# Semaphore waits of VectorE's SBUF operations for GpSimd's

## Chip, core and metric

One core of a Trainium2 chip runs the whole program in one launch. The metric is the device time in microseconds; 947.63 us is the median of three runs of the kernel before.

## What is computed

Decay attention over 4 x 8 heads, 576 positions and head size 64, and behind it two MoE-like blocks of 2304 tokens (512 to 2048 to 512), all in float32:

```python
scores = scale * q @ k.T + cum[i] - cum[j]      # cum = cumsum(log(clip(f))), causal
attn = softmax(scores); x = (attn @ v).reshape(2304, 512)
h = x @ w_in;  g = where(h >= 1, h, where(h <= -1, 0, (h + 1) ** 2 / 4));  x = g @ w_out
h = x @ w_in2; P = a0 + a1 h + a2 h^2 + a3 h^3
Q = 1 + |b0| |h| + |b1| h^2;  out = (P / (Q + 1e-6)) @ w_out2
```

## The kernel before

Matrix products run in float32r as three passes over high and low parts: each float32 operand is copied (high part, ScalarE) and the rest is subtracted (low part, VectorE or GpSimd). The first part of the program, to about 216 us, works through 16 pairs of heads with nine blocks of rows each: TensorE writes scores to PSUM (S), GpSimd masks the decay tile (`cb`, `affine_select`), VectorE adds it and takes maxima (P, nm), ScalarE takes exponentials, TensorE transposes (T), VectorE or ScalarE copies to SBUF (PT), TensorE multiplies by v (O), and GpSimd scales the result (`xa`, by R, which comes by DMA). Beside that, weights are converted from float64 words (`raw` to `wd`: one step of ScalarE, four of VectorE on SBUF) and the first columns of MoE 1 are computed as filler. From 216 to about 540 us MoE 1 runs, then MoE 2, which takes seven products for eight and evaluates its rational function on ScalarE, VectorE and GpSimd.

The order of all this is not that of the loops. Each piece is given as a `task` (key, engine or several ways, duration, function, dependencies, buffers). `plan` (L325) lists the tasks greedily on a clock of its own, and `emit` (L1200) calls their functions in that order, so each engine's queue has the order of the list. A task on VectorE that works on SBUF alone has the way "dvp"; this and GpSimd's "pool" are `SHARED`, and the planner lets only one of them run at a time (`port`). When it lists a GpSimd task whose start is under `NEAR` = 1.0 behind the end of the last "dvp" task, it notes this task in `behind` (L371 to L376). `emit` then adds a dependence with a semaphore: the first GpSimd instruction of the task waits for the last VectorE instruction of the other (L1206, L1207). `Kept` records what each of the two engines is given. In the other direction the kernel before has no such wait: a "dvp" task listed behind a GpSimd task starts as soon as its own data are there. The plan is made twice, for attention with the filler and for the rest.

```python
                if eng == "pool" and lastv and at - lastv[1] < NEAR:
                    behind[n] = lastv[0]
                elif eng == "dvp":
                    lastv = n, at + dur
```

The tasks named in the steps below: `w_steps` (L102, conversion, `wd`), `split_x_lo` (`xl`), the low parts of q and k (`ql`, `kl`, `lo`) and the diagonal copies (`qdh`, `qdl`, `diag`), `mask_fn` (`cb`), `r6` (`xa`), `split_g_lo` (`gl`) and `q_add` (`h<-h,us`). All of VectorE's and GpSimd's instructions bear line L26, that of the recording helper, so the rows are told apart by tiles.

Of the kernel before, what the change touches and what calls it, by code (L numbers as in the profile page):

```python
# [32 lines left out]
def kernel(ctx, tc, qT, kT, v, f, w_in1, w_out1, w_in2, w_out2, a, b, out):  # L33
    nc = tc.nc
    PE, ACT, DVE, POOL, SP = nc.tensor, nc.scalar, Kept(nc.vector), Kept(nc.gpsimd), nc.sync
# [259 lines left out]
    port = [T0]  # L295
# [6 lines left out]
    NEAR = 1.0  # L302
    behind, given_to = {}, {}
    after_it = mybir.DependencyInfo(mybir.DependencyClass.Sync, mybir.DependencyReason.SCHED_ONLY)
# [20 lines left out]
    def plan(first, wk):  # L325
        left, users = {}, {}
        for n in range(first, len(tasks)):
            users.setdefault(n, [])
            left[n] = 0
            for d in tasks[n][2]:  # L330
                if d >= first:
                    users.setdefault(d, []).append(n)
                    left[n] += 1
        ready = {n for n, k in left.items() if k == 0}
        order = []
        lastv = None
        while ready:
            best = None
            for n in ready:
                key, ways, deps, take, _ = tasks[n]  # L340
                free_at = 0.0
                ok = True
                need = {}
                for tag in take:
                    k = need[tag] = need.get(tag, 0) + 1
                    if len(bufs[tag]) < k:
                        ok = False
                        break
                    free_at = max(free_at, sorted(bufs[tag])[k - 1])
                if not ok:  # L350
                    continue
                choice = None
                for w, (eng, dur, _) in enumerate(ways):
                    at = max(clock[OF.get(eng, eng)], free_at, port[0] if eng in SHARED else 0.0)
                    eng = OF.get(eng, eng)
                    for d in deps:
                        e2 = by[d]
                        at = max(at, done[d] + (0.13 if e2 == eng and eng != "pe" else 0.0 if e2 == eng else LAT[e2]))
                    end = at + dur if len(ways) > 1 else 0.0
                    if choice is None or end < choice[0]:  # L360
                        choice = (end, at, w)

                turn = SWC if ways[0][0] == "pe" and shape.get(n) != at_shape[0] else 0.0
                cand = (choice[1] + turn + wk * key, key, n, choice[1], choice[2])
                if best is None or cand < best:
                    best = cand
            assert best, [(tasks[n][0], tasks[n][3]) for n in ready]
            _, key, n, at, w = best
            _, ways, _, take, free = tasks[n]
            eng, dur, fn = ways[w]  # L370
            if eng in SHARED:  # L371
                port[0] = at + dur
                if eng == "pool" and lastv and at - lastv[1] < NEAR:
                    behind[n] = lastv[0]
                elif eng == "dvp":
                    lastv = n, at + dur  # L376
            eng = OF.get(eng, eng)
            ready.discard(n)
            by[n] = eng
            for tag in take:  # L380
                bufs[tag].remove(min(bufs[tag]))
            if eng == "sp":
                for issue, moved in dur:
                    dma[0] = max(dma[0], at) + issue
                    dma[1] = max(dma[1], dma[0] + 0.64) + MOVE * moved
                clock[eng] = dma[0]
                done[n] = dma[1] + LAND
            elif eng == "init":
                done[n] = dur
            else:  # L390
                if eng == "pe" and shape.get(n) != at_shape[0]:
                    at_shape[0] = shape.get(n)
                    dur += SWT
                clock[eng] = at + dur
                done[n] = at + dur
            for tag in free:
                bufs[tag].append(done[n] + LAT[eng])
            order.append((at, n, fn))
            for u in users[n]:
                left[u] -= 1  # L400
                if left[u] == 0:
                    ready.add(u)
        assert len(order) == len(left), (len(order), len(left))
        order.sort(key=lambda t: t[:2])
        return [t[1:] for t in order]
# [737 lines left out]
    for size, kind, x, k in pieces:  # L1143
        key = FS + (FE - FS) * sofar / whole
        sofar += size
        n = CH[x]
# [27 lines left out]
    for kk in range(KD):  # L1174
        n = CH[FILL]
# [23 lines left out]

    def emit(order):  # L1200

        for n, fn in order:
            DVE.given, POOL.given = [], []
            fn()
            given_to[n] = DVE.given
            if n in behind and POOL.given and given_to[behind[n]]:  # L1206
                tc.add_manual_dep(POOL.given[0].ins, given_to[behind[n]][-1].ins.name, after_it, reason="port")  # L1207

    bufs.update({tag: [T0] * n for tag, n in N_BUF.items()})
    nudge(0)  # L1210
    order_ = plan(0, WK)
    emit(order_)
    filling = False
    att.close()
# [88 lines left out]
    for p, (m, x, fs) in enumerate(passes):  # L1303
        n = CH[x % NCH]
# [71 lines left out]
    n = QN  # L1376
# [102 lines left out]
    for n, x in enumerate(2 * s + 1 - c for s in range(NSUP) for c in range(2)):  # L1479
        for g in range(NF):  # L1480
# [3 lines left out]
            for d in range(QN // P):  # L1484
# [4 lines left out]
                if g == NF - 1:  # L1489
                    eng = ("act", "dve")[d % 2]  # L1490
                    o = task(key, eng, cost(eng, DM, "ps"), lambda x=x, d=d, eng=eng: out_copy(x, d, eng), (tout,), (("d", "d", "t2")[d],), (f"a{d}",))
                    task(key, "sp", ld(DM), lambda x=x, d=d: out_store(x, d), (o,), (), (("d", "d", "t2")[d],))
    nudge(first)
    order_ = plan(first, WKB)
    emit(order_)
    man.close()

# [45 lines left out]
```

## Time and profile before

| | us |
|---|---|
| median of three runs | 947.63 (947.1 to 947.81) |
| the profiled execution | 947.7 |
| its span in the trace | 946.0 |
| TensorE busy | 933.5 |
| VectorE busy | 740.0 |
| ScalarE busy | 704.4 |
| GpSimd busy | 442.9 |

The profiled execution's own time is 1.7 us longer than its span, and lies among the three runs. Matmuls are pipelined, so a busy TensorE says that it is never without one, not that it is at its peak. A VectorE or GpSimd row has the start and the length of an instruction; time in which an instruction has started and can't go on counts as its length, not as idle time.

### The profile page before, as it was taken

What the parts mean: (1) busy time and instruction counts of PE and PEld (TensorE: products, weight loads), DVE (VectorE), ACT (ScalarE), POOL (GpSimd) and SP (SyncE); (2) the same over time, 40 slices, a digit from 0 to 9 for tenths busy, and PEclk for the clock granted to TensorE, in tenths of its full rate; (3) what the DMA queues carried; (4) which work ended last, traced back from release to release, by engine and by line L of the source; (5) the groups of instructions that cost most, each with busy time, mean ns of one, the idle gap of its engine ahead of it and who ended that gap; (6) DMA issues with size and microseconds to landing.
All of it is one profiled execution on the core that took longest, in us unless ns stands there. A gap on an engine that the chain in (4) does not pass through costs nothing.

```text
span 946.0 us, 16654 instructions
## 1 busy us (share of the span) xinstructions
PE 933.5 (99%) x5172; PEld 789.2 (83%) x5172; DVE 740.0 (78%) x1614; ACT 704.4 (74%) x1568; POOL 442.9 (47%) x542
## 2 busy tenths in 40 slices
PE   9899999999999999999999999999999999999998
PEld 5666877778888888888998888989898989998986
DVE  7989789873866987897558598899988888888840
ACT  7899888875765654655556599889988898878752
POOL 3655733635565222131322076666655556455553
PEclk9999999999999999999999999999999999999999
DMA  8789799846554477686948865867434363434100
GB/s 258 235 267 278 238 300 282 255 164 205 178 178 150 164 261 270 196 289 221 325 144 273 267 196 189 263 227 256 140 136 147 139 234 121 141 131 151 34 34 34
DMA packets 107345, 188.55 MB, mean 199 GB/s; under 512 B 13092, under 2 KB 43188, under 8 KB 107256
## 3 DMA queue, kind: packets, MB, share of 16 engines
q1 hardware_dynamic: 107256, 187.48, 59.9%
q8 instruction: 41, 0.67, 0.3%
q14 instruction: 48, 0.39, 0.1%
HBM read 142.72 MB, written 44.71 MB: 198 GB/s over the span
## 4 chain that ended last, share of the span: by engine, by line
PE 88%; DMA 4%; DVE 4%; ACT 1%; issue 1%; SPq 1%; POOL 0%; DVEq 0%; POOLq 0%
PE b L1077 21%; PE h L799 20%; PE h L1051 19%; PE a L901 19%; PE T L573 3%; PE O L610 3%; PE a L890 2%; PE S L507 2%; DVE P L26 1%; DMA cb<-cd 1%; DMA vt<-in_v_dram 1%; DMA raw<-in_moe_w_in_dram 1%; DVE wd L26 1%; PE S L498 1%; DVE PT L26 1%
## 5 line engine op out<-in xcount | busy, mean ns | idle before, releaser
L26 POOL TENSOR_TENSOR gl<-t,gh 128x512 fp32r<-128x512 f32 (+2 forms) x125 | 140.1, 1127 | 216.4 <-ACT gh L815 87.3
L1077 PE MATMUL b<-w,gh 128*128 128x512 f32 x576 | 179.1, 392 | 0.0
L901 PE MATMUL a<-gh,w 128*128 128x512 f32 (+1 forms) x576 | 161.7, 366 | 0.0
L26 POOL TENSOR_TENSOR t<-t,t 128x384 f32<-128x384 f32 x96 | 97.4, 1018 | 97.2 <-ACT t L847 77.4
L1077 PEld LDWEIGHTS b<-w,gh 128*128 128x128 f32 x576 | 108.0, 188 | 21.1
L26 DVE SCALAR_TENSOR_TENSOR t<-h,t 128x512 f32<-128x512 f32 (+2 forms) x125 | 73.6, 600 | 61.1 <-ACT t L831 60.5
L799 PE MATMUL h<-xh,arena 128*128 128x512 f32 (+1 forms) x400 | 119.7, 368 | 0.0
L901 PEld LDWEIGHTS a<-gh,w 128*128 128x128 f32 x576 | 104.0, 189 | 17.1
L1077 PE MATMUL b<-w,gl 128*128 128x512 f32 x288 | 112.0, 389 | 0.0
L815 ACT CAST gh<-t 128x512 fp32r<-128x512 f32 (+2 forms) x125 | 68.7, 553 | 49.5 <-PE a L901 25.4
L901 PE MATMUL a<-gl,w 128*128 128x512 f32 (+1 forms) x288 | 105.3, 366 | 0.0
L26 DVE SCALAR_TENSOR_TENSOR wd<-raw,wd 128x512 int32<-128x512 int32 x128 | 98.1, 767 | 2.6
L561 ACT ACTIVATE P<-P,nm 128x576 f32<-128x576 f32 (+2 forms) x144 | 83.6, 582 | 13.9 <-DVE nm L26 13.4
L1051 PE MATMUL h<-arena,q 128*128 128x384 f32 x459 | 93.3, 337 | 0.0
L826 ACT ACTIVATE t<-h 128x512 f32<-128x512 f32 (+1 forms) x77 | 42.5, 551 | 61.6 <-PE h L799 60.0
L1051 PEld LDWEIGHTS h<-arena,q 128*128 128x128 f32 x459 | 81.4, 188 | 4.5 <-DVE h L26 1.2
L26 DVE TENSOR_SCALAR wd<-wd 128x512 f32<-128x512 f32 (+1 forms) x128 | 66.9, 523 | 21.6 <-ACT wd L109 19.9
L799 PEld LDWEIGHTS h<-xh,arena 128*128 128x128 f32 x400 | 73.1, 189 | 12.4
L799 PE MATMUL h<-xl,arena 128*128 128x512 f32 (+1 forms) x200 | 73.6, 368 | 0.0
L26 DVE CUSTOM_DVE_ANT_0 P<-S,cb 128x256 f32<-128x256 f32 (+1 forms) x135 | 62.5, 477 | 11.4 <-POOL cb L26 4.9
L26 POOL TENSOR_SCALAR_AFFINE_SELECT cb<-cb 128x128 f32<-128x128 f32 (+1 forms) x150 | 43.4, 301 | 59.5 <-DVE wd L26 26.7
L573 PE MATMUL T<-ident,P 128*128 128x128 f32 x400 | 63.7, 281 | 6.6 <-DVE PT L26 4.0
(170 smaller groups left out, 2213.7 us busy)
## 6 DMA issues: line engine op xcount, KB each, us to landing
q<-wqd SPq DMA_DIRECT2D x46, 512.0 KB, 3.6
raw<-in_moe_w_in_dram SPq DMA_DIRECT2D x32, 512.0 KB, 5.0
raw<-in_moe_w_out_dram SPq DMA_DIRECT2D x32, 512.0 KB, 4.2
arena<-wqd SPq DMA_DIRECT2D x26, 512.0 KB, 3.5
cb<-cd SPq DMA_DIRECT2D x15, 576.0 KB
xr<-xd SPq DMA_DIRECT2D x32, 256.0 KB, 3.4
wqd<-t SPq DMA_DIRECT2D x32, 256.0 KB, 3.7
wfd<-wd SPq DMA_DIRECT2D x26, 256.0 KB
```

Source lines behind the costliest of these rows:

```text
L26: self.given.append(getattr(self.engine, name)(*args, **kwargs))
L507: PE.matmul(ts[jj][:, to], qq[pp, bb_ * P:(bb_ + 1) * P] if x < 3 else qq[pp, :], kk_[pp, 0:(bb_ + 1) * P], start=(x == 0 and bb_ == b), s ...
L561: ACT.activation(p, p, AF.Exp, scale=-1.0, bias=nm[pr][:, pos:pos + 1], accum_out=ls[pr][:, COL[pos]:COL[pos] + 1])
L573: PE.transpose(ps[:, (c - c0) * P:(c - c0 + 1) * P], p[:, k0:k0 + P], ident[:])
L610: PE.matmul(o[pp, c_q:n], nat[pr, 2][:, c, pp], pt[:, c, j, c_q:n], start=(c == 0), stop=(c == ncs - 1),)
L799: PE.matmul(hps[g], ww[:, kk * P:(kk + 1) * P], xx[kk], start=(kk == 0 and y == 0), stop=(kk == KD - 1 and y == 2))
L815: ACT.copy(gt[g][0], mid[g][0][:, 0:n])
L826: ACT.activation(s[:, 0:n], hps[g], AF.Relu, scale=0.5, bias=0.5)
L890: PE.matmul(acc[x, d], ww[:, dd], gg, start=(part == 0 and g == gs[0]), stop=(part == 2 and g == gs[-1]))
L901: PE.matmul(acc[x, d], ww[:, dd], gg, start=(first and y == 0), stop=(last and y == 2))
L1051: PE.matmul(o, ww, xx, start=(new and i == 0 and z == 0), stop=(i == HQ - 1 and z == 2), skip_group_check=True,)
L1077: PE.matmul(acc[x, d], gg[:, dd], ww, start=(g == 0 and y == 0), stop=(g == NF - 1 and y == 2))
```

## The change

The planner keeps the last listed task of both shared ways, and each new shared task that starts under `NEAR` behind the last one of the other engine is noted in `behind`. What was done for GpSimd's tasks is now done for "dvp" tasks too: their first VectorE instruction waits by a semaphore for the last GpSimd instruction of the task noted. The planner's choices don't depend on `behind`, so the list is the same.

```diff
-        lastv = None
+        last = {}
...
             if eng in SHARED:
                 port[0] = at + dur
-                if eng == "pool" and lastv and at - lastv[1] < NEAR:
-                    behind[n] = lastv[0]
-                elif eng == "dvp":
-                    lastv = n, at + dur
+                other = last.get("dvp" if eng == "pool" else "pool")
+                if other and at - other[1] < NEAR:
+                    behind[n] = other[0]
+                last[eng] = n, at + dur
...
         for n, fn in order:
             DVE.given, POOL.given = [], []
             fn()
-            given_to[n] = DVE.given
-            if n in behind and POOL.given and given_to[behind[n]]:
-                tc.add_manual_dep(POOL.given[0].ins, given_to[behind[n]][-1].ins.name, after_it, reason="port")
+            given_to[n] = DVE.given or POOL.given
+            if n in behind and given_to[n] and given_to[behind[n]]:
+                tc.add_manual_dep(given_to[n][0].ins, given_to[behind[n]][-1].ins.name, after_it, reason="port")
```

## Rows read from the trace of the kernel before

**Rows 1.** The page, busy us, share of the span, and instructions of each engine:
```profile
PE 933.5 (99%) x5172; PEld 789.2 (83%) x5172; DVE 740.0 (78%) x1614; ACT 704.4 (74%) x1568; POOL 442.9 (47%) x542
```
**Rows 2.** Busy time by stretch: length, each engine, granted clock, DMA share, GB/s:
```profile
24.00:57.00 33.00, 30.48 (x255) 21.39 (x255) 31.66 (x106) 29.50 (x90) 21.30 (x43) 1.00 0.74 239
57.00:92.00 35.00, 31.66 (x269) 22.63 (x266) 31.45 (x103) 33.69 (x101) 19.55 (x41) 1.00 0.89 275
92.00:140.00 48.00, 47.75 (x343) 38.17 (x341) 40.22 (x127) 42.34 (x116) 25.31 (x48) 1.00 0.86 272
140.00:216.00 76.00, 75.35 (x569) 57.24 (x567) 62.32 (x188) 61.65 (x177) 34.41 (x69) 1.00 0.72 229
216.00:540.00 324.00, 324.00 (x1611) 275.95 (x1610) 231.20 (x406) 190.77 (x354) 106.01 (x88) 1.00 0.66 223
540.00:900.00 360.00, 360.00 (x1806) 324.98 (x1805) 314.18 (x612) 312.64 (x662) 207.20 (x202) 1.00 0.50 168
```
**Rows 3.** Who waited for whom, 24 to 92 us: us in total, times, longest:
```profile
PEld T L573 <- DVE PT L26: 4.1, 6, 1.1
...
PE T L573 <- DVE PT L26: 3.5, 6, 0.9
```
**Rows 4.** The same, TensorE and its weight loads, 92 to 216 us:
```profile
PE T L573 <- DVE PT L26: 0.5, 1, 0.5
...
PEld T L573 <- DVE PT L26: 1.3, 4, 0.7
```
**Rows 5.** The same, weight loads of TensorE, 216 us to the end:
```profile
PEld h L1051 <- DVE h L26: 1.2, 3, 0.4
```
**Rows 6.** By tile (wd, cb): instructions, ns least/median/most, first and last start, forms:
```profile
L26 DVE TENSOR_SCALAR wd<-wd x128: 366/426/1407, 22.3 to 513.6; 128x512 f32<-128x512 f32 x64, 128x512 int32<-128x512 int32 x64
L26 DVE SCALAR_TENSOR_TENSOR wd<-raw,wd x128: 631/692/1773, 25.5 to 514.8; 128x512 int32<-128x512 int32 x128
...
L26 POOL TENSOR_SCALAR_AFFINE_SELECT cb<-cb x150: 230/292/810, 17.2 to 202.8; 128x128 f32<-128x128 f32 x120, 64x64 f32<-64x64 f32 x30
```
**Rows 7.** Timelines, VectorE starting within GpSimd's operation: start us, length us, what:
```profile
22.10 0.40 POOL L26 TENSOR_TENSOR qdl<-ql,half 128x128 fp32r<-128x128 f32 x1
22.28 0.50 DVE L26 TENSOR_SCALAR wd<-wd 128x512 f32<-128x512 f32 x1
...
299.30 1.29 POOL L26 TENSOR_TENSOR gl<-t,gh 128x512 fp32r<-128x512 f32 x1
299.49 1.65 DVE L26 SCALAR_TENSOR_TENSOR wd<-raw,wd 128x512 int32<-128x512 int32 x1
...
780.00 0.55 DVE L26 TENSOR_TENSOR arena<-arena 128x384 fp32r<-128x384 f32 x1
```
**Rows 8.** The chain that ended last, around 46 us: start, length, what:
```profile
45.97 0.29 POOL cb L26
...
46.28 0.56 DVE P L26
```
**Rows 9.** Timelines, VectorE starting shortly before GpSimd's operation:
```profile
32.16 0.28 DVE L26 TENSOR_TENSOR qdl<-ql,half 128x128 fp32r<-128x128 f32 x1
32.24 0.34 POOL L26 TENSOR_SCALAR_AFFINE_SELECT cb<-cb 128x128 f32<-128x128 f32 x1 [0.61 <-DVE rt L26]
...
56.64 0.80 DVE L26 TENSOR_TENSOR ql<-qs,qh 128x576 fp32r<-128x576 f32 x1
56.77 1.05 POOL L26 TENSOR_SCALAR_AFFINE_SELECT cb<-cb 128x128 f32<-128x128 f32 x2
...
207.47 3.11 DVE L26 TENSOR_TENSOR xl<-xr,xh 128x512 fp32r<-128x512 f32 x3
207.82 1.61 POOL L26 TENSOR_TENSOR xa<-xa,R 128x576 f32<-128x576 f32 x1 [4.71 <-ACT po L419]
...
418.17 0.42 DVE L26 TENSOR_SCALAR wd<-wd 128x512 f32<-128x512 f32 x1
418.33 1.41 POOL L26 TENSOR_TENSOR gl<-t,gh 128x512 fp32r<-128x512 f32 x1 [6.22 <-DVE t_q L26]
```

## The prediction

> **What bounds the kernel now.** I read the page's busy times first. TensorE is busy for 933.5 of 946.0 us [rows 1], so only time in which TensorE stands, or is made to stand, can move the end. The second view is the busy time by stretch [rows 2]. From 216 to 900 us TensorE is busy without a break, 324 of 324 and 360 of 360 us, at a granted clock of 1.00. From 24 to 57 us it is busy for 30.5 of 33 us and from 57 to 92 us for 31.7 of 35, while VectorE works 31.7 of 33 and 31.5 of 35. From 92 to 216 us it is nearly full again (47.75 of 48, 75.35 of 76). The third view says who ends TensorE's waits. In 24 to 92 us, copies of VectorE out of PSUM do so 12 times for 7.6 us together [rows 3]; in 92 to 216 us for 1.8 us in the same two groups [rows 4]; behind 216 us the largest such wait is 1.2 us in three pieces [rows 5]. So one region is sensitive to a late VectorE: attention before 92 us. Afterwards TensorE has its filler (the first MoE) and deep buffers.
>
> **Which waits are added.** The ordering list comes out of the kernel before, and the change leaves it as it is. Read out, it holds 445 tasks of VectorE on SBUF; 208 of them stand behind a GpSimd task by less than the bound of 1.0 on the planner's clock. I looked up each of these pairs in the timelines of the two engines. In 108 the GpSimd operation was over when VectorE's started, so the wait finds its semaphore already raised and I cost it at nothing: it is read while VectorE works on the operation before. In 78 pairs GpSimd was in its operation when VectorE's started (first at 22.28, last at 780.00 us) [rows 7]. In 22 VectorE went first although it stands second in the list (first at 32.16, last at 418.17 us) [rows 9].
>
> **Price of a held pair.** Row 299.49 shows what happens without a semaphore. VectorE's operation lasts 1.65 us, where its like takes 0.692 in the median [rows 6], and ends at 301.14. GpSimd's ended at 299.30 + 1.29 = 300.59. So VectorE is made to wait inside its operation, and is done 0.55 us after GpSimd. With the semaphore it starts after GpSimd's end: for such a wait that exists already, the mask's end (45.97 + 0.29 = 46.26) is followed by VectorE's start at 46.28 [rows 8]. It then takes its full 0.69 and ends 0.71 us after GpSimd, 0.16 to 0.17 us later than now. The shorter kind gives the same: held, the operation at 22.28 ends at 22.78, some 0.28 after GpSimd's; with a wait it would be 0.02 + 0.426 = 0.45 [rows 6, 7]. The ends are 0.02 (nothing but the semaphore) and 0.17; I take 0.17, which both kinds give, and half of it where GpSimd had under 0.1 us left.
>
> The Trainium skill, page "SBUF — State Buffer", section "Who interferes with whom", says that the operation that starts first holds the shared ports for its whole instruction and the other fully blocks. This trace shows the blocking, but not the whole of it: the held operation needs 0.55 us behind GpSimd's end, not its 0.69. By the page the held pairs would cost only the semaphore and the sum below would be smaller (a rival, below). The same page, in "Summary: rules for kernel authors", advises to schedule whichever is off the critical path as the second one; that speaks against a change that puts GpSimd ahead where VectorE bounds.
>
> **Price of a reversed pair.** Here GpSimd is held now, and VectorE would be. At 32.16 VectorE starts, at 32.24 the mask; a mask takes 0.29 [rows 6, 9]. With the wait VectorE starts at 32.24 + 0.29 + 0.02 = 32.55, 0.4 us later. At 56.64 it is 56.77 + 0.29 + 0.02, again 0.4 us: two masks are merged in that row, of which the first is the one in the way. Where GpSimd's operation is long, as at 207.47 (xl against xa) or 418.17 (wd against gl), the first operation loses 1.4 to 1.8 us, but the next one of VectorE is held now by that same GpSimd operation and would no longer be, so the queue as a whole loses 0.4 to 0.6. What is queued behind each waiting operation is VectorE's own: maxima out of S, copies of T to PT, max/min of h; TensorE waits for these.
>
> **The sum.**
> - 24 to 57 us: five held pairs that count (31.38 to 54.43) x 0.17 = 0.85, two reversed (32.16, 56.64) x 0.4 = 0.8; 1.65 us on VectorE. It has 33 - 31.7 = 1.3 us of idle time there [rows 2]; I let three quarters pass: 1.2.
> - 57 to 92 us: eight held, four of them with little left, 4 x 0.17 + 4 x 0.08 = 1.0; two reversed, 0.9; together 1.9. VectorE has 3.5 us idle, and ScalarE is the busier one (33.7 of 35). One third passes: 0.6.
> - 92 to 216 us: 17 held, some 2.1 us, and 7 reversed at 0.4 to 0.8, some 4.0; together 6.1. TensorE's waits for VectorE are 1.8 us of 124 [rows 4], so filler covers nearly all; I let 6% through: 0.4.
> - 216 us to the end: 46 held and 11 reversed, about 12 us on VectorE. TensorE has no gap to lengthen, and VectorE is idle for 93 of 324 us in the first MoE and 46 of 360 in the second [rows 2]. Cover: the four banks of h and the three of g. If that cover were gone, each would cost its 0.17 to 0.6. I take 0.
> The total is +2.2 us: span 946.0 to 948.2, the profiled execution 947.7 to 949.9, and on the median of 947.63 it gives 949.8. Nothing else is moved: no DMA, no order, no shape. The three shares are my choice between nothing and everything, which would be 0 and +9.7 us (without the part behind 216 us).
>
> **Rivals.**
> - Absorbed. The delays fall into VectorE's own idle time (1.3 + 3.5 us before 92 us) and the waits of TensorE that end on ScalarE stay what they were: +0.4, 948.0. It decides if at least three quarters of the 3.6 us before 92 us vanish. For it: from 57 to 92 us ScalarE is the busier one and the DMA share is 0.89 [rows 2], so something else may end last. Against it: VectorE at 96% in 24 to 57 us, with 7.6 us of TensorE's waits ended by its copies [rows 2, 3].
> - GpSimd gains. In the 22 reversed pairs a mask or a split now takes up to 0.81 instead of 0.29, or 1.41 instead of 1.29 [rows 6, 7, 9]; the change gives this back, 5 us on GpSimd in all. If half of it lay on the path and VectorE's delays did not, 2.5 us: 945.1. Against it: GpSimd is busy for less than half of the span [rows 1], and the maximum that needs a freed mask stands in VectorE's queue behind the operation that would now wait.
> - A stand-off. In a fixed order VectorE now waits for a GpSimd operation that itself waits, as xa at 207.82 did for 4.71 us [rows 9]. If one or two such meet VectorE in attention at full length, +2.2 + 4.7 makes 954.5. For it: GpSimd's inputs come from DMAs and ScalarE. Against it: only 22 of the 208 pairs are reversed, and in those shown GpSimd starts 0.08 to 0.35 us after VectorE (0.35 for xa, although it had stood 4.71 us).
> - Held pairs are free. If a held operation has done nothing when GpSimd ends, the semaphore costs it only 0.02 us, and the three stretches come to 0.7 + 0.4 + 0.3 = 1.4 us: 949.0. Rows 299.49 and 22.28, done 0.55 and 0.28 us after GpSimd, speak against it [rows 7]. This is what the Trainium skill's page "SBUF — State Buffer" would lead to.
> - No waits: the added dependence may be there already through others, and nothing changes: 947.6.
>
> **How the numbers follow.** A measurement of this kernel tells about 0.2% from no change, that is 1.9 us. The forecast gets 0.48, with its own range from 948.8 to 951.6; 0.36 of it lies over the bound and 0.12 within. Absorbed has 0.26, free held pairs 0.03, no waits 0.05 (all within 0.2%), the stand-off 0.12 (slower) and GpSimd's gain 0.06 (faster). So faster 0.06, same 0.46, slower 0.48. The range reaches from 946.7, a little below no change, to 953.5: under it lies most of GpSimd's gain, above it the worse half of the stand-offs.
>
> **What would show it.** In the profile after, VectorE's operations on SBUF at 0.42 and 0.69 us have no long kinds of 1.3 to 1.7 us any more, and idle time ended by GpSimd stands before them; mean of wd falls towards 0.69. Masks of 0.6 to 0.8 us are gone. TensorE is still without a gap behind 216 us, and what is lost is lost before, by waits for PT in 24 to 92 us. I am wrong if VectorE's busy time keeps its held operations (no waits), if TensorE has gaps in the MoE (no cover), or if attention ends at the same place (absorbed) or earlier.

## The result and the profile after

The changed kernel takes 954.5 us (median of four runs, 954.02 to 955.61), against 947.37 in the runs beside it: the ratio is 1.0074, with a 95% interval of 1.0061 to 1.0086, or 7 us slower. The forecast was 949.8, with 953.5 as the upper end. The profiled execution took 954.41 us, its span is 952.7.

The page of the changed kernel, busy times; it answers to [rows 1]:

```profile
PE 936.8 (98%) x5172; PEld 789.0 (83%) x5172; DVE 711.2 (75%) x1614; ACT 705.8 (74%) x1568; POOL 438.0 (46%) x542
```

VectorE is busy 29 us less than before, though it does the same work: time that counted as length of held operations is now idle time in front of them. The view by tile shows that no operation of the conversion (`wd`) and no mask (`cb`) is held any more (compare the largest values with [rows 6]):

```profile
L26 DVE TENSOR_SCALAR wd<-wd x128: 366/427/430, 22.3 to 520.2; 128x512 f32<-128x512 f32 x64, 128x512 int32<-128x512 int32 x64
L26 DVE SCALAR_TENSOR_TENSOR wd<-raw,wd x128: 629/691/703, 25.4 to 521.4; 128x512 int32<-128x512 int32 x128
...
L26 POOL TENSOR_SCALAR_AFFINE_SELECT cb<-cb x150: 233/294/307, 17.2 to 207.4; 128x128 f32<-128x128 f32 x120, 64x64 f32<-64x64 f32 x30
```

Busy time by the same stretches as in [rows 2]:

```profile
24.00:57.00 33.00, 30.17 (x250) 21.04 (x249) 29.47 (x104) 28.91 (x89) 20.30 (x42) 1.00 0.74 233
57.00:92.00 35.00, 30.73 (x262) 22.10 (x260) 30.27 (x101) 33.19 (x99) 18.31 (x41) 1.00 0.87 274
92.00:140.00 48.00, 46.87 (x331) 36.49 (x330) 38.74 (x122) 40.62 (x106) 25.01 (x47) 1.00 0.78 245
140.00:216.00 76.00, 74.55 (x571) 56.47 (x571) 63.17 (x199) 64.25 (x186) 32.49 (x70) 1.00 0.73 243
216.00:540.00 324.00, 323.05 (x1603) 274.50 (x1603) 204.27 (x402) 189.57 (x349) 105.17 (x89) 1.00 0.65 219
540.00:900.00 360.00, 359.92 (x1794) 322.79 (x1794) 310.36 (x604) 311.00 (x658) 205.54 (x200) 1.00 0.52 173
```

TensorE has lost some tenths of a microsecond or more in every stretch but the last (0.08), and for the first time has gaps behind 216 us, where it had none. Four of its waits from 92 us on are new: three for GpSimd, the two longest among them, and one for a copy of ScalarE. Waits of TensorE, 92 us to the end:

```profile
PE h L799 <- POOL w L26: 1.0, 1, 1.0
PE h L799 <- POOL tail L26: 0.8, 1, 0.8
PE T L573 <- ACT PT L419: 0.5, 1, 0.5
...
PE S L498 <- POOL qdl L26: 0.2, 1, 0.2
```

Both traces hold the same 5172 matmuls in the same order (but for two neighbouring pairs of score products, whose recorded starts lie within 0.3 us), so their starts can be laid side by side. The table gives how late TensorE is against the kernel before, at times of the kernel before (medians of some 40 to 60 matmuls around them, us). The columns e1 to e10 are the experiments below. Up to half a microsecond at 24 us is the start of the run, which differs between executions, and is to be taken off.

| at us | changed | e1 | e2 | e3 | e4 | e8 | e9 | e10 |
|---|---|---|---|---|---|---|---|---|
| 24 | 0.0 | -0.6 | 0.0 | 0.3 | -0.4 | -0.5 | -0.1 | 0.0 |
| 90 | 1.2 | 0.6 | -0.2 | 0.4 | 0.5 | 0.7 | 0.0 | -0.1 |
| 104 | 2.7 | 2.0 | -0.2 | 1.1 | 1.3 | 0.9 | 1.1 | -0.1 |
| 140 | 3.4 | 2.8 | -0.1 | 1.2 | 1.3 | 1.8 | 1.1 | -0.1 |
| 215 | 4.3 | 3.6 | -0.2 | 1.4 | 1.6 | 2.7 | 1.1 | -0.2 |
| 262 | 4.7 | 4.2 | 0.2 | 1.4 | 2.9 | 3.1 | 1.0 | 0.2 |
| 320 | 5.8 | 4.2 | 1.0 | 1.5 | 3.6 | 3.1 | 1.9 | 0.2 |
| 700 | 6.7 | 4.1 | 1.8 | 1.5 | 4.4 | 4.0 | 1.9 | 0.2 |

So of the 6.7 us of the span, 1.2 to 1.4 are lost before 92 us, 2.9 from there to 216 us, and 2.4 behind it.

### Where the lost time enters

Three products show it best. In the kernel before (timelines of GpSimd and TensorE, start, length, what), each takes a tile of GpSimd just after it is done:

```profile
100.00 1.29 POOL L26 TENSOR_TENSOR w<-wd,w 128x512 fp32r<-128x512 f32 x1 [0.44 <-ACT w L147]
...
101.54 0.48 PE L799 MATMUL h<-xh,w 128*128 128x512 f32 x1
...
254.08 1.47 POOL L26 TENSOR_TENSOR gl<-t,gh 128x512 fp32r<-128x512 f32 x1
...
255.91 0.39 PE L901 MATMUL a<-gl,w 128*128 128x512 f32 x1
...
311.89 1.47 POOL L26 TENSOR_TENSOR tail<-wd,tail 128x512 fp32r<-128x512 f32 x1 [0.43 <-ACT gh L815]
...
313.25 0.62 PE L901 MATMUL a<-gh,w 128*128 128x512 f32 x2
313.71 0.39 PE L799 MATMUL h<-xh,tail 128*128 128x512 f32 x1
```

Call the time from the end of GpSimd's operation to the start of the product its lead. It is 101.54 - 101.29 = 0.25 us, 255.91 - 255.55 = 0.36 and 313.71 - 313.36 = 0.35. No gap of TensorE shows that. The same places in the changed kernel:

```profile
102.89 1.27 POOL L26 TENSOR_TENSOR w<-wd,w 128x512 fp32r<-128x512 f32 x1 [0.61 <-DVE wd L26]
...
104.22 0.50 PE L799 MATMUL h<-xh,w 128*128 128x512 f32 x1 [1.05 <-POOL w L26]
...
259.10 1.30 POOL L26 TENSOR_TENSOR gl<-t,gh 128x512 fp32r<-128x512 f32 x1
...
260.45 0.50 PE L901 MATMUL a<-gl,w 128*128 128x512 f32 x1
...
318.06 1.27 POOL L26 TENSOR_TENSOR tail<-wd,tail 128x512 fp32r<-128x512 f32 x1 [0.60 <-DVE wd L26]
...
317.93 0.61 PE L901 MATMUL a<-gh,w 128*128 128x512 f32 x2
319.38 0.50 PE L799 MATMUL h<-xh,tail 128*128 128x512 f32 x1 [0.84 <-POOL tail L26]
```

At the third place TensorE comes 317.93 - 313.25 = 4.68 us late. The tile is done at 319.33 instead of 313.36, 5.97 us late, that is 1.29 later than TensorE; the lead takes 0.35 of it and 0.94 remains, and TensorE starts the product 5.67 us late, 0.99 more than it came with. (The product itself and the next lose 0.1 more.) Lateness less lead is the loss.

How VectorE and GpSimd get that late is seen just ahead. VectorE in the changed kernel:

```profile
305.36 0.69 DVE L26 SCALAR_TENSOR_TENSOR wd<-raw,wd 128x512 int32<-128x512 int32 x1 [1.11 <-POOL gl L26]
307.53 0.43 DVE L26 TENSOR_SCALAR wd<-wd 128x512 f32<-128x512 f32 x1 [1.48 <-POOL gl L26]
309.42 0.43 DVE L26 TENSOR_SCALAR wd<-wd 128x512 int32<-128x512 int32 x1 [1.47 <-POOL tail L26]
309.88 1.42 DVE L26 SCALAR_TENSOR_TENSOR wd<-raw,wd 128x512 int32<-128x512 int32 x2
...
314.57 1.42 DVE L26 SCALAR_TENSOR_TENSOR wd<-raw,wd 128x512 int32<-128x512 int32 x2
...
317.49 0.43 DVE L26 TENSOR_SCALAR wd<-wd 128x512 f32<-128x512 f32 x1 [0.90 <-POOL gl L26]
```

The first is the operation of [rows 7] that was done at 301.14; it is done at 306.05, 4.91 us late, where TensorE is 4.68 late. The second is done 0.2 later still (307.96 instead of 302.86, 5.10 us late). The third is the VectorE task of a reversed pair; the two operations behind it end at 309.88 + 1.42 = 311.30 instead of 305.75, 5.55 late, so it costs the queue 0.4 to 0.5.

GpSimd takes this lateness over by its own waits, those that the kernel before has already, and not by its data. The tail at 318.06 reads a weight whose last step on VectorE is done at 314.57 + 1.42 = 315.99, and that weight's high part, which ScalarE copies until 316.64:

```profile
316.02 0.62 ACT L147 CAST tail<-wd 128x512 fp32r<-128x512 f32 x1 [0.35 <-DVE wd L26]
```

GpSimd's operation before it, a gl, ends at 317.45. Still the tail starts at 318.06, behind "0.60 <-DVE wd". That wd, from 317.49 to 317.92, is the first VectorE step (the clip) of the next weight, which the tail doesn't read; the tail stands behind it in the planner's list and waits for it by order, as in the kernel before. And this wd had itself waited for the gl ("0.90 <-POOL gl"), by one of the new waits. So lateness goes round: from GpSimd by the new wait to VectorE, with the price of a held pair on top, and by the old wait back to GpSimd. The low part w at 102.89 is let go in the same way, 0.61 us behind the mask before it, by a wd of the next weight that had waited 1.12 us for that mask.

The rest of the loss enters in smaller steps. From 92 to 216 us these are some 0.35 us at 109, 0.2 at 116, 0.26 at 175.6 (the wait for qdl) and 0.4 at 191.5 (the wait for ScalarE's PT). In the second MoE there are four, of 0.15 to 0.3 us, at 557, 619, 633 and 667 us. No conversion of weights is in these four: weight loads of TensorE wait there for VectorE's tailh twice, its t and its osb. Of these only tailh stands in the list of before, once with 0.3 us; in the changed kernel:

```profile
PEld h L1051 <- DVE tailh L26: 0.8, 2, 0.4
```

### The profile page after: what moved, and what is told of

It is laid out like the page before. It is cut to its first block, busy times and chain, and to the rows that moved or that the text cites. A ratio compares the mean times of both kernels' runs of the same rounds, so it can differ in the third digit from the quotient of the medians.

```text
span 952.7 us, 16648 instructions
## 1 busy us (share of the span) xinstructions
PE 936.8 (98%) x5172; PEld 789.0 (83%) x5172; DVE 711.2 (75%) x1614; ACT 705.8 (74%) x1568; POOL 438.0 (46%) x542
## 5 line engine op out<-in xcount | busy, mean ns | idle before, releaser
L26 DVE SCALAR_TENSOR_TENSOR wd<-raw,wd 128x512 int32<-128x512 int32 x128 | 87.7, 687 | 11.7 <-POOL arena L26 3.2
L1051 PE MATMUL h<-arena,q 128*128 128x384 f32 x459 | 93.5, 337 | 0.0
L26 DVE TENSOR_SCALAR wd<-wd 128x512 f32<-128x512 f32 (+1 forms) x128 | 54.2, 424 | 52.2 <-POOL gl L26 31.9
L26 POOL TENSOR_SCALAR_AFFINE_SELECT cb<-cb 128x128 f32<-128x128 f32 (+1 forms) x150 | 40.8, 284 | 62.1 <-DVE wd L26 28.6
```

The source lines that it names most:

```text
L26: self.given.append(getattr(self.engine, name)(*args, **kwargs))
L1051: PE.matmul(o, ww, xx, start=(new and i == 0 and z == 0), stop=(i == HQ - 1 and z == 2), skip_group_check=True,)
```

## The experiments

All of them but the last are the changed kernel with a filter on its waits, so the order, the work and GpSimd's own waits are the same unless said otherwise. Each time is the median of 4 to 12 runs, taken beside runs of the kernel before.

### Halves of the program

```diff
-                if other and at - other[1] < NEAR:
+                if other and at - other[1] < NEAR and (eng == "pool" or first == 0):    # e1; e2: first > 0
```

> VectorE's waits are kept in the first plan alone (attention with the filler), 98 of the 208 pairs; the MoE half is that of the kernel before. Theory A (lateness of VectorE at the waits runs on through GpSimd to products that have little lead): in the changed kernel TensorE is 4.3 us late at 216 us of the 6.7 at its end, so +4.3 us: 951.7. Theory B (a fixed price of 0.17 us for each held pair, half of which passes): 32 of 78 held pairs lie here, +2.9: 950.3. Theory C (every added wait costs as an instruction, met or not): 98 of 208, +3.4: 950.8. If the MoE's lateness comes only from what attention hands over, the whole +7 stays: 954.4.

Measured: 951.72 us, ratio 1.0040 (1.0026 to 1.0054).

> VectorE's waits are kept in the second plan alone (both MoEs), 110 of the 208 pairs. Theory A: +2.4 us, what TensorE loses behind 216 us in the changed kernel (0.4 at 256, 1.0 to 1.1 at 314, 0.9 in the second MoE): 949.8. Theory B: 46 of 78 held pairs, +4.1: 951.5. Theory C: +3.7: 951.1. If the MoE's lateness is only handed over from attention: 947.4.

Measured: 949.82 us, ratio 1.0022 (1.0014 to 1.0031).

4.2 and 2.3 us make 6.5 of the 7.1. The waits behind 216 us cost time by themselves, although TensorE had no gap there; these 2.3 us aren't lateness handed over from attention. The table has e2 losing at the places of the changed kernel: 0.4 at 256, 0.85 at 314 and 0.8 from 545 to 700 us. Both times came out as theory A had them; that took the sizes from the changed kernel's trace, so it shows that the halves add up, and not yet why. They add up in total and not place by place: in e1, which has no new waits behind 216 us, 0.65 us enter between 215 and 262 us, most of it at a product that waits for VectorE's xl (low part of x), and at that product the changed kernel loses nothing.

### Kinds of pairs

```diff
+    ONLY = {...}     # task numbers: e3 the 22 reversed, e4 the 78 held, e5 the 108 met pairs
...
+                if other and at - other[1] < NEAR and (eng == "pool" or n in ONLY):
```

> Only the 22 VectorE tasks wait that started ahead of their GpSimd operation in the trace of the kernel before. Theory A: these are the long waits (0.4 to 2 us each), so they make most of the loss: +4 to +6 us, 951.5 to 953.5. Theory B: they are no held pairs, +1 us or less: 948.4. Theory C: 22 of 208, +0.8: 948.2.

Measured: 949.19 us, ratio 1.0014 (1.0005 to 1.0023).

> Only the 78 VectorE tasks wait that started within their GpSimd operation in the trace of the kernel before. Theory A: about 0.17 us each on VectorE, little of which meets a product with no lead: +1 to +2 us, 948.4 to 949.4. Theory B: all of it, +7: 954.4. Theory C: 78 of 208, +2.7: 950.1.

Measured: 952.27 us, ratio 1.0046 (1.0033 to 1.0058).

> Only the 108 VectorE tasks wait whose GpSimd operation was over in the trace of the kernel before. If a wait that is already met costs nothing, 947.5 as before, within 1 us. If each costs as an instruction, 108 of 208 of the loss, +3.7: 951.2. The runs with reversed and held pairs alone came to +1.7 and +4.8; what is left of +7.1 is 0.6, so no more than that is expected.

Measured: 947.75 us, ratio 1.0005 (0.9996 to 1.0013).

Theory A was wrong in what it made of the kinds: the few long waits are not what costs most. The many held pairs alone cost 4.8 us, which is two thirds of the loss, and the reversed ones alone 1.7. Theory B was nearer in that, though it left the reversed pairs too little. A wait that is met costs nothing that can be measured, which rules theory C out. With held pairs alone, TensorE waits for the same two tiles as in the changed kernel (its lines are eight further down, because of the list):

```profile
PE h L807 <- POOL w L26: 0.5, 1, 0.5
...
PE h L807 <- POOL tail L26: 0.4, 1, 0.4
PE h L807 <- DVE xl L26: 0.3, 1, 0.3
```

The last line is a wait that the changed kernel doesn't have. At two products that wait for xl, at 232 and 240 us, e4 loses 0.7 us. So the sizes by kind are those of each kind alone, and not shares of the changed kernel's 7.1.

The price itself could be read for all held pairs with more than 0.1 us of GpSimd's operation left, 65 of them: VectorE's operation ends 0.18 us later behind GpSimd's end than before (median; 0.284 to 0.461 for the short kind). The price on VectorE is much the same everywhere; what it costs at the end isn't.

### Two places, left out and alone

```diff
+    SPARED = {...}   # e8: 15 task numbers;  e9: the same 15 in ONLY
...
+                if other and at - other[1] < NEAR and (eng == "pool" or n not in SPARED):
```

> The changed kernel, with 15 of its 208 waits left out: those of VectorE tasks that stood at 93.5 to 101 us and 296 to 313 us in the trace of the kernel before, just ahead of two weights' low parts that TensorE took 0.25 and 0.35 us after they were done. If the loss comes in where a product has little lead, it falls by the two steps seen in the changed kernel, 1.3 and 1.1 us: 952.1. If it is spread over all waits evenly, 15 of 208 or 0.5 us: 954.0. If lateness built up earlier decides, the two places stay late and it is 954 as well.

Measured: 952.27 us, ratio 1.0052 (1.0039 to 1.0064).

> The kernel before with 15 of VectorE's 208 waits, those left out in the run before (tasks that stood at 93.5 to 101 us and 296 to 313 us). If the lateness that meets the two low parts is made on the spot, the time rises by what leaving them out gave back: +2.0 us, of which 1.2 at 101.5 us and 0.8 at 313.7 us; 949.4. If it takes the lateness built up by all waits ahead, the two places keep their lead of 0.25 and 0.35 us and the time stays within 0.5 us of 947.4.

Measured: 949.58 us, ratio 1.0020 (1.0011 to 1.0028).

Leaving out 15 of 208 waits gives back 2.2 us, and the same 15 alone cost 2.05. In the table e8 has no step at 101 and none at 314 us, e9 has these two (1.1 and 0.85) and no other. Waits of TensorE in e9 (lines four further down); its two others are those of the kernel before:

```profile
PE h L803 <- POOL w L26: 0.9, 1, 0.9
...
PE h L803 <- POOL tail L26: 0.5, 1, 0.5
```

So most of the lateness that meets these two products is made by the waits of the 8 us ahead of the first (93.5 to 101) and the 17 us ahead of the second (296 to 313). Alone they cost 1.1 and 0.85 us at the products, where the changed kernel loses 1.3 and 1.1; little of what the waits before had built up is left by then.

### The other waits of the MoE half

```diff
+                if other and at - other[1] < NEAR and (eng == "pool" or first > 0 and n not in SPARED):
```

> VectorE's waits in the second plan alone (110 pairs), but for the 39 of tasks that stood at 244 to 257, 296 to 313 and 545 to 668 us, ahead of the five places at which TensorE lost time in the run with all 110. If a wait costs only ahead of a product with little lead, the other 71 waits cost nothing: within 0.5 us of the kernel before, 947.4. If each of the 110 costs its share of +2.3, 71 of them cost 1.5: 948.9.

Measured: 947.75 us, ratio 1.0002 (0.9993 to 1.0010).

Of the 110 waits behind 216 us, 71 cost nothing that can be measured. 38 of these are met pairs, which cost nothing in e5 either; 26 held and 7 reversed pairs say something new. The 2.3 us come from the 39 that were left out. At 256 and 314 us these stand ahead of products whose leads were measured, 0.36 and 0.35 us; in the second MoE they are spread from 545 to 668 us, and no lead was measured there. Weight loads of TensorE behind 216 us wait nearly as before, for `h` above all, and what GpSimd ends among their longest is 0.2 us:

```profile
PEld h L1056 <- DVE h L26: 1.2, 3, 0.4
...
PEld a L906 <- POOL gl L26: 0.2, 1, 0.2
```

### The waits of GpSimd

```diff
-                if other and at - other[1] < NEAR:
+                if other and at - other[1] < NEAR and False:            # e6;  e7: and eng == "dvp"
```

> Neither engine waits for the other by order: GpSimd's waits of the kernel before are gone too. If a wait costs its engine more than being held does, in GpSimd's case too, this is a little faster than before: -0.5 to -1.5, 946.5. If GpSimd's waits keep long GpSimd operations from getting ahead of VectorE's (each would hold VectorE by up to 1.3 us), it is slower: +2 to +5, 951.

Measured: 957.0 us, ratio 1.0103 (1.0089 to 1.0117).

> VectorE waits for GpSimd as in the changed kernel; GpSimd's waits for VectorE are gone. If the loss runs round a loop (VectorE late, so GpSimd late by its own waits, so VectorE late), the loss against the kernel without any waits falls to about half: +3 to +4 over that kernel. If it is only the sum of VectorE's own waits, it stays at +7 over it.

Measured: 961.47 us, ratio 1.0141 (1.0125 to 1.0156).

> The kernel before, in which GpSimd's task waits for VectorE's if it is listed within 2.0 instead of 1.0 behind its end; VectorE has no waits. The kernel without any waits is 9.7 us slower than before, so GpSimd's waits pay. If more of them pay too: -0.5 to -2 us, 946. If those listed further behind are met when GpSimd comes to them, nothing: 947.4. If they make GpSimd late ahead of a product with little lead, as VectorE's do: +1 to +2, 949.

Here VectorE has no waits, and the kernel before is changed in one line:

```diff
-                if eng == "pool" and lastv and at - lastv[1] < NEAR:
+                if eng == "pool" and lastv and at - lastv[1] < 2 * NEAR:
```

Measured: 947.52 us, ratio 0.9997 (0.9988 to 1.0005).

GpSimd's waits of the kernel before are worth 9.7 us. Without them VectorE is busy for 759.0 us instead of 740.0, held that much longer. By TensorE's starts, 4.2 us of e6's lateness enter before 90 us and 5.6 between 320 and 700 us, where it waits among others for VectorE's h (1.5 us) and t (0.8). The same instrument helps on the engine that has time (GpSimd, busy 47%) and hurts on the other; that this is the reason was not tried apart. Part of the 9.7 us is something else: from 47 to 54 us of e6 the granted clock was 0.53 (below), and in e7 it was 0.76 there.

VectorE's waits cost 4.5 us where GpSimd has none, against 7.1 where it has. The trace of e7 fits the round described above at the two products: TensorE is 3.74 us late just before and just after 101.54, and 7.35 around 313.71, so it loses nothing at either, and both low parts are let go by ScalarE's copies and come 0.30 and 0.28 us ahead of their products. But the kernels differ in all their timing, so how much of the difference of 2.6 us is this round stays open. Waits of GpSimd for pairs between 1.0 and 2.0 apart (e11) change nothing that can be measured.

## Why the prediction was wrong

- **Direction: right; size: wrong.** Slower was forecast, by 2.2 us; it is 7.1, and the range ended 1 us too early.
- **The price of a held pair: right.** 0.17 us were forecast, 0.18 measured. The semaphore is seen 0.033 us after GpSimd's end in the median held pair, not 0.02, and the operation then takes its full length. The Trainium skill, page "SBUF — State Buffer", section "Who interferes with whom", has the second operation fully blocked until the first is done. The runs differ on this point: a held operation is done 0.28 us behind GpSimd where it needs 0.43 alone, so about 0.14 us of it passes during the hold, or the hold ends that much ahead of GpSimd's recorded end; the rows don't tell these apart. With the semaphore those 0.14 us are given up, which is most of the price.
- **The price of a reversed pair: right.** 0.4 to 0.6 us were forecast for the queue; behind the pair at 302.89 it is 0.46 (5.55 us late, 5.09 ahead of it). No theory of a stand-off is needed: the longest wait of VectorE for GpSimd in the list of waits is 3.3 us, in front of a wd that waits for gl, and the 4.7 us of the rival did not occur: the wait for xa that it was read from is 2.1 us. That rival's time, 954.5, is met by chance.
- **GpSimd's gain: right in size, and not on the path.** Some 5 us were named; GpSimd is busy for 4.9 us less (442.9 to 438.0), and the kernel is slower all the same.
- **Before 92 us: right, a little too high.** 1.8 us were forecast, 1.2 to 1.4 measured. The copies to PT end more of TensorE's waits, as they should: in 24 to 93 us

```profile
PEld T L573 <- DVE PT L26: 5.2, 6, 1.5
...
PE T L573 <- DVE PT L26: 4.3, 5, 1.3
```

  together 9.5 us instead of 7.6 [rows 3]. These sums, and the prediction's, count the wait of a product and that of its weight load for the same copy twice; TensorE's products alone wait 4.3 us instead of 3.5.
- **92 to 216 us: the first step that failed.** "I let 6% through", 0.4 us of 6.1; it was 2.9 us. The share was taken from the waits that TensorE has now. Nearly half of the loss, 1.3 us, enters at one product, whose weight's low part had a lead of 0.25 us; the way to it is that of the next point.
- **216 us to the end: the second.** "TensorE has no gap to lengthen ... I take 0"; it was 2.4 us, of 12 on VectorE. The cover named there, the banks of h and the buffers of g, may have been enough for much of it: 26 held and 7 reversed pairs cost nothing (e10). But I took VectorE's own results for the only way from VectorE to TensorE. The other goes through GpSimd's queue: VectorE waits for GpSimd (new), GpSimd's low part, or the operation just ahead of it, waits for VectorE by order (as before), and the product for the low part. All that covers the product is the time by which the low part is early, and at 313.71 us that was 0.35. This way costs 1.5 of the 2.4 us, at 256 and 314 us. The other 0.9 enter in the second MoE on the way that the prediction did name, at weight loads that wait for VectorE's tailh, t and osb, so there the cover didn't hold; the leads there weren't measured. An engine without a gap says that nothing was late, and doesn't say by how much it was early.
- **Met pairs: right.** 108 waits, nothing measurable (e5). (The list holds 453 tasks of VectorE on SBUF; the 445 of the prediction are those that stand behind some GpSimd task.)
- **What stays open:** which single pairs make the 1.6 us that attention loses elsewhere from 92 to 216 us, and the 0.9 of the second MoE; and 0.6 us between the changed kernel and the kinds of pairs run alone (6.5 of 7.1), which is no more than the intervals leave.

## What to carry to other kernels

Before a wait is costed at nothing because the bounding engine has no gaps, measure the lead: for each product the time from the end of its last input to its start. At the products measured here, where the lead was shorter than the lateness that the waits made in the 8 to 17 us ahead of it, the difference went to the end in full; 33 held and reversed waits elsewhere were free. Follow lateness through waits by order as well as through data: two engines that wait for each other hand it round. Here a wait by order paid on the engine that had time, and one that replaced a hold in hardware cost the 0.14 us that the held operation was ahead, plus 0.03 for the semaphore.

## What was not expected of the hardware

Without GpSimd's waits (e6) TensorE stood for a moment in attention, and ran at about half its clock for some microseconds after that. Busy time by stretch in e6, TensorE first, granted clock third from the end:

```profile
44.00:47.00 3.00, 2.16 (x15) 1.12 (x11) 2.93 (x6) 1.29 (x5) 1.85 (x2) 1.00 0.92 249
47.00:54.00 7.00, 6.52 (x32) 5.78 (x34) 4.63 (x17) 4.54 (x13) 4.42 (x12) 0.53 0.54 200
54.00:60.00 6.00, 6.00 (x50) 3.79 (x50) 5.71 (x21) 6.00 (x20) 1.73 (x4) 0.99 0.54 178
```

TensorE was busy for 2.16 of 3.00 us from 44 to 47 us, a gap of 1.2 us ended at 47.5, and TensorE then had a granted clock of 0.53, close to 1.2 GHz of its 2.4, to 54 us. Against the kernel before, it was 2.3 us late when that gap was over and 4.7 us late at the end of the slow stretch, so by an estimate some 2.4 us of e6's loss (10.8 us in the span of this execution) are clock and not waits. In e7 the same gap stands at the same place. The gap alone doesn't decide it: in the changed kernel TensorE stood for 1.3 us in one piece, to 59.5 us, and was busy for as much of the 3 us around it,

```profile
56.00:59.00 3.00, 2.16 (x27) 1.53 (x23) 2.25 (x8) 3.00 (x10) 1.92 (x4) 1.00 0.80 231
```

and its clock is 1.00 there and in every stretch shown, so none of its 7 us are of that kind. What made the difference stays open.
